# An attention-plus-MLP kernel on one core: the masked attention rebuilt in 64x64 quadrants of the matmul array

## The chip, the cores and the metric

The kernel runs on one core of one Trainium2 chip. The metric is the device time of one execution in microseconds (us), and a lower time is better. Times are medians of several executions. "Span" is the length of the one execution that the profiler recorded, a few us shorter than the time.

The profile names the engines PE (TensorE, matrix products), PEld (its weight loads), DVE (VectorE), ACT (ScalarE), POOL (GpSimd, which here issues the loads) and SP (SyncE, which here issues stores and transposes). `SPq` is SP's queue of DMA issues.

## The reference

There are eight batches with eight heads, 576 positions and a head size of 64. Heads 0 to 3 see a band of 32 keys, and heads 4 to 7 see every 32nd key. The result feeds two dense layers with a rational function between them.

```python
rel = pos[:, None] - pos[None, :]
mask_local   = (rel >= 0) & (rel < 32)                                   # heads 0..3
mask_strided = (rel >= 0) & (pos[None, :] % 32 == pos[:, None] % 32)     # heads 4..7
attn = softmax(where(mask, q @ k.T / 8, -1e9)) @ v
x = attn.transpose(0, 2, 1, 3).reshape(4608, 512)
h = x @ w_in                                                             # 512 -> 2048
P = a[0] + a[1] * h + a[2] * h**2 + a[3] * h**3
Q = 1.0 + abs(b[0]) * abs(h) + abs(b[1]) * h**2
out = (P / (Q + 1e-6)) @ w_out                                           # 2048 -> 512, float32
```

## The kernel before

The program records every operation with its engine, dependencies, a cost and a priority key. A list scheduler then fixes one static order for each engine. A ready operation with the lowest key goes first.

```python
for u in op.users:
    hop = 0.03 if (u.eng == e and op.group is None) else self.HOP    # gap before a dependent operation
    u.ready = max(u.ready, op.end + hop)
```

The tokens are cut into nine chunks of 512. Eight chunks hold the first 512 positions of one batch each, and the ninth holds the 64 left over from every batch. Attention of a batch passes in eleven rounds through one score tensor, `psS`, of two banks of PSUM, the memory where this program's matmuls put their results. Some rounds turn q and k with an identity product. The others add a mask (identity times mask, 128 columns wide) to the score products.

```python
psS = Pa("psS", [128, 2, 512], F32);  psA = Pa("psA", [128, 8, 128], F32)
psH = [Pa(f"psH{i}", [128, 512], F32) for i in range(3)];  psO = Pa("psO", [128, 512], F32)

def score_round(key, msk, width, qks, exps, deps, e_slot):
    for j in range(2):
        makers.append(mm(psS[:, j, 0:width], IDN[:, :], msk[:, 0:width], True, False))
    for (o, l, r) in qks:
        makers.append(mm(o, l, r, False, False))
    o1 = add("PE", makers, [deps, s_free[0], cons], cost, key)     # cons: all constants, one semaphore
```

The attention output goes to `XR`, is turned by a DMA transpose into `XT`, and feeds the first dense layer (`psH`). ACT copies that to `HB`. Nine DVE operations and two ACT ones make the rational function for a group of 512-token blocks. The second dense layer (`psO`) follows, then a copy to `OS` and the stores.

```python
for kk in range(NK1):
    r = XT[c % NXT][:, kk, :]
    makers.append(mm(psH[hi][:, :], Win[:, kk, 128 * f:128 * f + 128], r, kk == 0, kk == NK1 - 1))
o1 = add("PE", makers, [xt_ev[c], g1.ops, h_free[hi]], 4 * mmc(512), key)
# ... nine DVE operations; the polynomial's are a chain, each needs the one before:
d5 = add("DVE", ... t3 = t3 * hb ..., [d4], ctt, key + 0.04)
d6 = add("DVE", ... t3 = t3 + a1 ..., [d5], cts, key + 0.05)
d7 = add("DVE", ... t3 = t3 * hb ..., [d6], ctt, key + 0.06)
```

The softmax here doesn't subtract the row's maximum and nothing guards it: scores larger than these inputs give would overflow.

Of the kernel before, what the change touches and what calls it, by code (L numbers as in the profile page):

```python
# [4 lines left out]
dt = mybir.dt  # L5
# [6 lines left out]
STRIDE = 32  # L12
# [47 lines left out]
class Program:  # L60
# [32 lines left out]
    def schedule(self):  # L93
# [22 lines left out]
        while left:  # L116
# [34 lines left out]
            for u in op.users:  # L151
                hop = 0.03 if (u.eng == e and op.group is None) else self.HOP
                u.ready = max(u.ready, op.end + hop)
                u.nwait -= 1
                if u.nwait == 0:
                    heapq.heappush(future[u.eng], (u.ready, u.idx, u))
# [108 lines left out]
def bass_strided_sparse_attn__then__act_rational_pade_kernel(nc, q, k, v, moe_w_in, moe_w_out, moe_a, moe_b, out):  # L265
# [6 lines left out]
    NP = S // 4  # L272
    HL = 4
# [5 lines left out]
    P = 36.0  # L279
# [6 lines left out]
    qm = [A(f"qm{i}", [128, 256], BF) for i in range(NN)]  # L286
    km = [A(f"km{i}", [128, 256], BF) for i in range(NN)]
    sT = A("sT", [128, 2, 2, 4, NP], BF)
    qL = A("qL", [128, 2, S], BF)
    kL = A("kL", [128, 2, S], BF)  # L290
    NV = 2
    vt = [A(f"vt{i}", [128, 4, 4, VS], BF) for i in range(NV)]
    v4 = [A(f"v4{i}", [64, 4, VS], BF) for i in range(NV)]
    w4 = [A(f"w4{i}", [128, 4, VS], BF) for i in range(NV)]
    vs = [A(f"vs{i}", [128, 4, 4, VS], BF) for i in range(NV)]
    NE = 2
    EL1 = [[A(f"EL1_{i}_{p}", [128, 2, 4, 128], BF) for p in range(2)] for i in range(NE)]
    EL2 = [A(f"EL2_{i}", [128, 2, 2, 4, 4, 32], BF) for i in range(NE)]
    EL3 = [A(f"EL3_{i}", [64, 2, 2, 4, 32], BF) for i in range(NE)]
    ESW = 8 * NP + 64  # L300
    ES = [A(f"ES_{i}", [128, 2, ESW], BF) for i in range(NE)]
# [6 lines left out]
    XT8 = A("XT8", [128, NK1, B * 128], BF)  # L308
    NHB = 2
    HB = [A(f"HB{i}", [128, G, CH], BF) for i in range(NHB)]  # L310
    NT3 = 6
# [3 lines left out]
    NO = 4  # L315
    OS = [A(f"OS{i}", [128, 512], F32) for i in range(NO)]
# [4 lines left out]
    ML1 = A("ML1", [128, 512], BF)  # L321
    ML2 = A("ML2", [128, 384], BF)
    MS1 = A("MS1", [128, 3 * NP], BF)
    MS2 = A("MS2", [128, 2 * NP + 64], BF)
    IDN = A("IDN", [128, 128], BF)

    Pa = nc.alloc_psum_tensor
    psS = Pa("psS", [128, 2, 512], F32)
    psA = Pa("psA", [128, 8, 128], F32)
    NHP = 3  # L330
    psH = [Pa(f"psH{i}", [128, 512], F32) for i in range(NHP)]
    psO = Pa("psO", [128, 512], F32)


    ar = np.arange(128)
    part = np.arange(128)
    d1 = (4 * (ar % 32) + ar // 32)[None, :] - part[:, None]
    m1 = np.where((d1 >= 0) & (d1 < STRIDE), 0.0, NEG)
    ml1 = np.tile(m1, (1, 4))
    ml2 = np.full((128, 2, 4, 4, 8), NEG)  # L340
    ml3 = np.full((128, 2, 4, 16), NEG)
    for g in range(4):
        for i in range(16):
            dd = 4 * i + g - part
            ok = (dd >= 0) & (dd < STRIDE) & (part < 64)
            ml3[ok, :, g, i] = 0.0
            dd = 128 + 4 * i + g - part
            ok = (dd >= 0) & (dd < STRIDE)
            if i < 8:
                ml2[ok, :, :, g, i] = 0.0  # L350
            else:
                assert not ok.any()
    ml2 = np.concatenate([ml3.reshape(128, -1), ml2.reshape(128, -1)], axis=1)
    dp = np.arange(NP)[None, :] - part[:, None]
    ms = np.where((dp >= 0) & (dp % 8 == 0), 0.0, NEG)
    ms1 = np.tile(ms, (1, 3))
    iq = np.arange(16)[None, :]
    ik = (part % 32)[:, None]
    mlo = np.where((ik < 16) & (iq >= ik) & ((iq - ik) % 8 == 0), 0.0, NEG)
    ms2 = np.concatenate([np.tile(ms, (1, 2)), np.tile(mlo, (1, 4))], axis=1)  # L360
# [7 lines left out]
    nch = [0]  # L368
# [3 lines left out]


    gC = chan("c_const").group()
    cons = []
    for dst, arr, nm in ((IDN, np.eye(128), "c_idn"), (ML1, ml1, "c_ml1"), (ML2, ml2, "c_ml2"),
                         (MS1, ms1, "c_ms1"), (MS2, ms2, "c_ms2")):
        c = const(nm, arr)
        cons.append(add("SP", (lambda e, dst=dst, c=c: e.dma_start(dst.bitcast(dt.uint16)[:, :], c[:, :])),
                        [], 0.1, -900, gC, 0.1))  # L380
    cst_np = np.zeros((1, 2), np.float32)
    cst_np[0, 0] = 1.0 + 1e-6
    cst_c = nc.inline_tensor(cst_np, name="c_cst")
    cons.append(add("SP", lambda e: e.dma_start(
# [6 lines left out]
        coef[:, 6:8], coef[:, 4:6], -1.0, coef[:, 4:6], op0=Alu.mult, op1=Alu.max), [cons], 0.2, -400)  # L391
# [6 lines left out]

    ini = {}

    def memset(buf, ap, val, key=-800.0, eng="DVE", cost=0.3):
        o = add(eng, (lambda e, ap=ap, val=val: e.memset(ap, val)), [ini[id(buf)][-1]] if id(buf) in ini else [],
                cost, key)
        ini.setdefault(id(buf), []).append(o)

    for i in range(NV):
        memset(vt[i], vt[i][:, :, :, 64:65], 1.0)
        memset(vs[i], vs[i][:, :, :, 64:65], 1.0)
        memset(v4[i], v4[i][:, :, 64:65], 1.0)
        memset(w4[i], w4[i][:, :, 64:65], 1.0)  # L410
    for i in range(NE):
        memset(EL2[i], EL2[i].rearrange("x a q t g c -> x (a q t g c)"), 0.0, cost=1.2)
        memset(EL3[i], EL3[i].rearrange("x a q g c -> x (a q g c)"), 1.0)


    ch_n = [[chan(f"c_n{x}{i}") for i in range(NN)] for x in "qk"]
    ch_v = [chan(f"c_v{i}") for i in range(NV)]
    ch_x = [chan(f"c_x{i}") for i in range(NX)]
    ch_w1 = chan("c_w1")
    ch_w2 = chan("c_w2")  # L420
    ch_o = [chan(f"c_o{i}") for i in range(NO)]
    n_free = [[[] for _ in range(NN)] for _ in range(2)]
# [3 lines left out]
    g1 = ch_w1.group()  # L426
    g2 = ch_w2.group()

    def load_win():
        add("POOL", (lambda e: e.dma_start(Win[:, :, :], w_in.rearrange("(a p) f -> p a f", p=128))),  # L430
            [], 1.0, -940.0, g1, 12.0)

    def load_wout():
        add("POOL", (lambda e: e.dma_start(Wout[:, :, :], w_out.rearrange("(f p) o -> p f o", p=128))),
            [], 1.3, -920.0, g2, 12.0)

    def loads(b):

        key = (b - 2.5) * P if b > 1 else -1000.0 + 50 * b
        i = b % NN  # L440
        for x, src, dst, dsm in ((0, q, qn, qm), (1, k, kn, km)):
            g = ch_n[x][i].group()
            add("POOL", (lambda e, src=src, dst=dst, b=b, i=i: e.dma_start(
                dst[i][:, :, :], src[b, :, 0:512, :].rearrange("h (p g) d -> p h (g d)", g=4))),
                [n_free[x][i]], 0.9, key + x, g, 3.8)
            add("POOL", (lambda e, src=src, dsm=dsm, b=b, i=i: e.dma_start(
                dsm[i][:, :], src[b, :, 512:576, :].rearrange("h (p g) d -> h p (g d)", g=4))),
                [n_free[x][i]], 0.7, key + x + 0.1, g, 0.5)
            n_ev[x, b] = g.ops
        gv = ch_v[b % NV].group()  # L450
        i = b % NV
        base = [v_free[i], ini[id(vt[i])], ini[id(vs[i])], ini[id(v4[i])], ini[id(w4[i])]]
        key = (b - 1.9) * P if b > 1 else key + 5
        for h in range(4):
            add("POOL", (lambda e, b=b, i=i, h=h: e.dma_start(  # L455
                vs[i][:, h, :, 0:64],
                v[b, 4 + h, 0:512, :].rearrange("(p g) d -> p g d", g=4))),
                base, 0.85, key, gv, 1.1)
        for g in range(4):
            add("POOL", (lambda e, b=b, i=i, g=g: e.dma_start(  # L460
                w4[i][32 * g:32 * g + 16, :, 0:64],
                v[b, 4:8, 512:576, :].rearrange("h (p g) d -> g p h d", g=4)[g])),
                base, 0.65, key, gv, 0.15)
        for h in range(4):
            add("POOL", (lambda e, b=b, i=i, h=h: e.dma_start(  # L465
                vt[i][:, :, h, 0:64],
                v[b, h, 0:512, :].rearrange("(t p) d -> p t d", p=128))),
                base, 0.85, key, gv, 1.1)
        add("POOL", (lambda e, b=b, i=i: e.dma_start(
            v4[i][:, :, 0:64],  # L470
            v[b, 0:4, 512:576, :].rearrange("h s d -> s h d"))),
            base, 0.7, key, gv, 0.5)
        v_ev[b] = gv.ops


    s_free = [None]
    a_free = [None]
# [10 lines left out]
    def mmc(n):  # L488
        return max(n / 2.4, 28.0) * 1e-3 + 0.003

    def score_round(key, msk, width, qks, exps, deps, e_slot):
        makers = []
        nq = 0
        for j in range(2):
            makers.append(mm(psS[:, j, 0:width], IDN[:, :], msk[:, 0:width], True, False))
        for (o, l, r) in qks:
            makers.append(mm(o, l, r, False, False))
            nq += mmc(r.free_size())
# [3 lines left out]
        s_free[0] = o2  # L502
        return o2

    q_free = [[]]

    def evac(eng, dst, src, dep, key, n):
        if eng == "ACT":
# [414 lines left out]
```

## Time and profile before

The time before was 436.72 us (three runs, 436.19 to 440.19). The span has three parts:

| part | from | to | length |
|---|---|---|---|
| prologue: until the first dense matmul (`psH<-XT,Win`) | 0 | 69.9 | 69.9 |
| body: until the last operation of the rational function | 69.9 | 419.3 | 349.4 |
| tail: last dense products, copies, stores | 419.3 | 437.7 | 18.4 |

These lines are from the page of the kernel before: busy time by engine, then busy tenths in 40 slices of the span, with the clock that the throttle granted to TensorE.

```profile
PE 363.3 (83%) x3392; PEld 175.3 (40%) x3392; DVE 326.8 (75%) x307; ACT 307.1 (70%) x339; POOL 105.9 (24%) x142
PE   0446748896989699999999998999997999997950
DVE  2201301989799849499969999799988999999940
PEclk9999999985999999999999999999999999999995
```

PE and DVE both near 9 through most of the body mean that two engines are close to their limits at once. DVE does almost nothing in the first six slices.

The clock row misleads at its start. This trace's record of the clock begins at 73.0 us, and the view counts time without a record as full speed. The matmul starts tell otherwise. Up to 73 us, matmuls of 128 columns start 107 ns apart and the dense ones of 512 columns 427 ns; later it is 56 and 216 ns. So TensorE ran at half speed in the prologue, and the 1.00 in the first line below is not measured.

The windows view of the kernel before gives the same for the prologue and the body. Its columns are the stretch, its length, busy us of PE, PEld, DVE, ACT and POOL (with instructions), the clock, the DMA share and GB/s.

```profile
0.00:69.90 69.90, 32.77 (x428) 17.48 (x429) 12.06 (x31) 20.40 (x21) 40.15 (x61) 1.00 1.56 161
69.90:419.30 349.40, 326.88 (x2954) 156.31 (x2948) 313.40 (x274) 285.47 (x316) 65.78 (x81) 0.98 0.46 62
```

The chain of waits of the kernel before shows why the prologue is long. Each line is a start, a duration and what the chain passed through.

```profile
4.24 9.21 DMA coef<-in_moe_b_dram
13.59 1.02 PE psS L486 x8
14.64 1.24 DVE sT L510
16.01 1.03 PE psS L486 x8
17.06 1.03 ACT sT L509
...
44.29 8.45 DMA XT<-XR
...
68.33 1.64 PE psS L486 x17
69.97 3.33 PE psH L486 x8
```

The first score matmul waits for a small constant, because all constants share one semaphore. After that PE and an evacuation take turns on `psS` until 69.97, with an 8.45 us transpose between.

The timeline of the kernel before shows the tail. The line's columns are start, duration, engine, source line, operation, tiles and count.

```profile
421.05 14.87 SPq L806 DMA_DIRECT2D out_dram<-OS  x32
421.96 1.03 PE L486 MATMUL psS<-Wout,T 128*128 128x512 bf16 x4
```

The last matmul starts at 421.96, and 32 store issues keep the queue busy for 14.87 us.

### The profile page before, as it was taken

What the parts mean: (1) busy time and instruction counts of PE and PEld (TensorE: products, weight loads), DVE (VectorE), ACT (ScalarE), POOL (GpSimd) and SP (SyncE); (2) the same over time, 40 slices, a digit from 0 to 9 for tenths busy, and PEclk for the clock granted to TensorE, in tenths of its full rate; (3) what the DMA queues carried; (4) which work ended last, traced back from release to release, by engine and by line L of the source; (5) the groups of instructions that cost most, each with busy time, mean ns of one, the idle gap of its engine ahead of it and who ended that gap; (6) DMA issues with size and microseconds to landing.
All of it is one profiled execution on the core that took longest, in us unless ns stands there. A gap on an engine that the chain in (4) does not pass through costs nothing.

```text
span 437.7 us, 7910 instructions
## 1 busy us (share of the span) xinstructions
PE 363.3 (83%) x3392; PEld 175.3 (40%) x3392; DVE 326.8 (75%) x307; ACT 307.1 (70%) x339; POOL 105.9 (24%) x142
## 2 busy tenths in 40 slices
PE   0446748896989699999999998999997999997950
PEld 0223423442345255455544543555443444443420
DVE  2201301989799849499969999799988999999940
ACT  1152243768899777979698889898888499959520
POOL 9960091261101911900480009000000000000000
PEclk9999999985999999999999999999999999999995
DMA  8999999383503994952497228313111210112112
GB/s 120 175 184 196 172 120 130 46 60 40 70 13 74 179 40 61 151 81 67 57 103 121 49 49 80 57 31 77 28 41 31 67 49 25 48 26 54 42 32 65
DMA packets 92227, 34.03 MB, mean 78 GB/s; under 512 B 66080, under 2 KB 87072, under 8 KB 92192
## 3 DMA queue, kind: packets, MB, share of 16 engines
q0 software_dynamic: 62112, 18.37, 45.5%
q1 hardware_dynamic: 30080, 15.16, 16.6%
q8 instruction: 26, 0.43, 0.4%
q14 instruction: 9, 0.07, 0.1%
HBM read 37.17 MB, written 9.44 MB: 106 GB/s over the span
## 4 chain that ended last, share of the span: by engine, by line
PE 59%; DVE 16%; ACT 13%; DMA 6%; issue 2%; SPq 1%; DVEq 0%
PE psH L486 25%; PE psO L486 17%; PE psS L486 14%; ACT kL L509 4%; PE psA L486 4%; DMA XT<-XR 4%; DVE T L784 3%; DVE T L779 2%; ACT UU L765 2%; DMA coef<-in_moe_b_dram 2%; DVE UU L759 2%; DVE T L775 2%; ACT ES L582 1%; DVE T L777 1%; ACT HB L745 1%
## 5 line engine op out<-in xcount | busy, mean ns | idle before, releaser
L486 PE MATMUL psH<-XT,Win 128*128 128x512 bf16 x576 | 145.9, 391 | 4.1 <-DMA XT<-XR 2.1
L486 PE MATMUL psO<-Wout,T 128*128 128x512 bf16 x528 | 132.6, 380 | 9.2 <-ACT OS L849 7.0
L745 ACT ACTIVATE HB<-psH 128x512 bf16<-128x512 f32 x144 | 83.6, 604 | 36.1 <-PE psH L486 34.4
L486 PEld LDWEIGHTS psH<-XT,Win 128*128 128x128 bf16 x576 | 54.9, 100 | 70.6 <-issue 6.4
L765 ACT ACTIVATE UU<-UU,cst 128x2048 bf16<-128x2048 bf16 x36 | 71.9, 2001 | 8.1 <-DVE UU L759 8.1
L486 PEld LDWEIGHTS psO<-Wout,T 128*128 128x128 bf16 x528 | 47.1, 98 | 66.4 <-ACT OS L849 11.5
L768 ACT ACTIVATE UU<-UU 128x2048 bf16<-128x2048 bf16 x36 | 69.0, 1918 | 0.1
L455 POOL DMA_DIRECT2D vs<-in_v_dram x32 | 28.1, 884 | 103.1 <-PE psA L486 102.9
L784 DVE TENSOR_TENSOR T<-T,UU 128x4096 bf16<-128x4096 bf16 (+1 forms) x20 | 41.3, 2067 | 6.0 <-ACT UU L768 6.0
L775 DVE TENSOR_TENSOR T<-T,HB 128x4096 bf16<-128x4096 bf16 (+1 forms) x20 | 41.5, 2075 | 0.3
L759 DVE TENSOR_TENSOR UU<-UU,T 128x4096 bf16<-128x4096 bf16 (+1 forms) x20 | 41.5, 2073 | 0.3
L779 DVE TENSOR_TENSOR T<-T,HB 128x4096 bf16<-128x4096 bf16 (+1 forms) x20 | 41.4, 2071 | 0.2
L510 DVE CAST sT<-psS 128x1024 bf16<-128x1024 f32 (+1 forms) x16 | 13.2, 822 | 38.1 <-PE psS L486 38.1
L582 ACT ACTIVATE ES<-psS 128x864 bf16<-128x864 f32 (+1 forms) x24 | 20.3, 845 | 18.7 <-PE psS L486 18.5
L680 DVE TENSOR_TENSOR XR<-psA,RC 128x512 bf16<-128x512 f32 x40 | 27.5, 688 | 2.9 <-DMA XT<-XR 2.7
L753 DVE TENSOR_SCALAR T<-HB 128x4096 uint16<-128x4096 uint16 (+1 forms) x20 | 22.2, 1109 | 8.9 <-ACT HB L745 8.9
L678 DVE RECIPROCAL RC<-psA 128x8 f32<-128x8 f32 x40 | 8.2, 204 | 25.8 <-PE psA L486 25.7
L849 ACT ACTIVATE OS<-psO 128x512 f32<-128x512 f32 x33 | 19.7, 597 | 10.6 <-PE psO L486 10.1
L486 PE MATMUL psS<-ML,IDN 128*128 128x512 bf16 (+1 forms) x48 | 15.9, 418 | 13.5 <-ACT kL L509 9.0
L486 PE MATMUL psS<-IDN,qn 128*64 128x128 bf16 (+1 forms) x192 | 12.4, 254 | 17.5 <-DMA coef<-in_moe_b_dram 13.6
L465 POOL DMA_DIRECT2D vt<-in_v_dram x32 | 26.9, 870 | 0.0
L772 DVE TENSOR_SCALAR T<-HB,coef 128x4096 bf16<-128x4096 bf16 (+1 forms) x20 | 25.4, 1269 | 0.2
(77 smaller groups left out, 395.6 us busy)
## 6 DMA issues: line engine op xcount, KB each, us to landing
out_dram<-OS SPq DMA_DIRECT2D x128, 64.0 KB, 1.7
qn<-in_q_dram POOLq DMA_DIRECT2D x8, 512.0 KB, 6.4
kn<-in_k_dram POOLq DMA_DIRECT2D x8, 512.0 KB, 8.3
vs<-in_v_dram POOLq DMA_DIRECT2D x32, 64.0 KB, 6.0
vt<-in_v_dram POOLq DMA_DIRECT2D x32, 64.0 KB, 3.9
Win<-in_moe_w_in_dram POOLq DMA_DIRECT2D x1, 2048.0 KB, 14.7
Wout<-in_moe_w_out_dram POOLq DMA_DIRECT2D x1, 2048.0 KB, 26.3
out_dram<-OS SPq DMA_DIRECT2D x32, 32.0 KB, 1.7
```

The costliest lines, as they stand in the source:

```text
L455: add("POOL", (lambda e, b=b, i=i, h=h: e.dma_start(vs[i][:, h, :, 0:64], v[b, 4 + h, 0:512, :].rearrange("(p g) d -> p g d", g=4))), base ...
L465: add("POOL", (lambda e, b=b, i=i, h=h: e.dma_start(vt[i][:, :, h, 0:64], v[b, h, 0:512, :].rearrange("(t p) d -> p t d", p=128))), base, ...
L486: return lambda e: e.matmul(out_ap, l, r, start=start, stop=stop, skip_group_check=True)
L680: o3 = add("DVE", (lambda d, rc=rc, x=x: d.tensor_tensor(x.rearrange("x (h d) -> x h d", h=8), psA[:, :, 0:64], rc[:, :, :].to_broadcast([ ...
L745: o2 = add("ACT", (lambda a, hb=hb, hi=hi, fi=fi: a.activation(hb[:, fi, :], psH[hi][:, :], AF.Copy)), [o1, hb_free[ig % NHB]], 0.6, key - 30)
L759: d3 = add("DVE", (lambda d, gn=gn, u=u, t3=t3: d.tensor_tensor(u[:, 0:gn, :], u[:, 0:gn, :], t3[:, 0:gn, :], op=Alu.mult)), [d2], ctt, ke ...
L765: ln = add("ACT", (lambda a, u=u, sl=sl: a.activation(u[:, sl, :], u[:, sl, :], AF.Ln, bias=cst[:, 0:1], scale=1.0)), [d3, cons], 0.28 + H ...
L768: ex = add("ACT", (lambda a, u=u, sl=sl: a.activation(u[:, sl, :], u[:, sl, :], AF.Exp, scale=-1.0)), [ln], 0.28 + HG * CH * 0.000833, key ...
L772: d4 = add("DVE", (lambda d, gn=gn, hb=hb, t3=t3: d.tensor_scalar(t3[:, 0:gn, :], hb[:, 0:gn, :], a_ap[3], a_ap[2], op0=Alu.mult, op1=Alu. ...
L775: d5 = add("DVE", (lambda d, gn=gn, hb=hb, t3=t3: d.tensor_tensor(t3[:, 0:gn, :], t3[:, 0:gn, :], hb[:, 0:gn, :], op=Alu.mult)), [d4], ctt ...
L779: d7 = add("DVE", (lambda d, gn=gn, hb=hb, t3=t3: d.tensor_tensor(t3[:, 0:gn, :], t3[:, 0:gn, :], hb[:, 0:gn, :], op=Alu.mult)), [d6], ctt ...
L784: d9 = add("DVE", (lambda d, gn=gn, t3=t3, u=u: d.tensor_tensor(t3[:, 0:gn, :], t3[:, 0:gn, :], u[:, 0:gn, :], op=Alu.mult)), [d8, lns], c ...
```

## The change

The change rebuilds attention in 64x64 quadrants of the array and rearranges what surrounds it. Its parts are these:

- Masks are products of one-hot matrices of 64 rows, four quadrants a set, in place of 128-wide masks.
- q and k are turned by PSUM transposes in bf16, so that one copy takes 2048 elements.
- PSUM becomes four sets of two banks (S, A, H, O). Batch 0 and batch 1 spread over all of them.
- Loads are reordered and split: strided heads first, `Win` in two halves, a semaphore for each constant.
- The token order in `XT` changes, so the dense layer reads its moving operand in short runs.
- Groups at the start and end get smaller, one `T3` buffer goes, stores go by 64 partitions, and the scheduler's gap for the same engine goes from 0.03 to 0.

```diff
-                hop = 0.03 if (u.eng == e and op.group is None) else self.HOP
+                hop = 0.0 if (u.eng == e and op.group is None) else self.HOP
...
-    P = 36.0
+    P = 34.0
+    SB, AB = 1.4, 0.0
...
-    NT3 = 6
+    NT3 = 5
...
-    psS = Pa("psS", [128, 2, 512], F32)
-    psA = Pa("psA", [128, 8, 128], F32)
-    psH = [Pa(f"psH{i}", [128, 512], F32) for i in range(NHP)]
-    psO = Pa("psO", [128, 512], F32)
+    PS = {n: Pa("ps" + n, [128, 2, 512], F32) for n in "SAHO"}
...
+    def quads(ps, col, w, mcol, rhs, start):
+        for c in range(2):
+            for r in range(2):
+                res.append(mm(ps[64 * c:64 * c + 64, r, col:col + w],
+                              MK[64 * r:64 * r + 64, mcol + 64 * c:mcol + 64 * c + 64], rhs[r], start, False))
...
+                            makers.append(tp(pb[:, x, o:o + 128], T[:, 4 + h, 128 * gh:128 * gh + 128], IDN[:, :]))
...
-        return [4, 4, 8] if c == 0 else [8, 4, 4] if c == NCH - 1 else [8, 8]
+        return [2, 2, 4, 8] if c == 0 else [8, 4, 2, 2] if c == NCH - 1 else [8, 8]
...
-                        r = XT[c % NXT][:, kk, :]
+                            if kk < 2:
+                                r = xt[:, kk, :].rearrange("x (s c r) -> x c s r", c=8, r=4)
+                            else:
+                                r = xt[:, kk, :].rearrange("x (s c r) -> x c s r", c=8, r=32)
...
-                        dst[g], OS[osl][64 * bb + 16 * g:64 * bb + 16 * g + 16, :])), [ev], 0.45, key - 60, go, 0.1)
+                src = OS[osl][64 * z:64 * z + 64, e_, :]
...
+                    dst = out[r0:r0 + 64, :].rearrange("(i g) o -> g i o", g=4)
```

## The prediction

> **What bounds the kernel now.** The span is 437.7 us, in three parts (timeline view).
> 1. *Prologue, 0 to 69.9 us*, before the first dense matmul (group psH<-XT,Win). PE is busy 33 of the first 70 us, DVE 12 (windows view). The first score matmul starts at 13.59, released by the coefficient load, because all constants share one semaphore. Eleven rounds per batch then pass one by one through the single two-bank score tensor: batch 0 to about 41, batch 1, ahead of dense work on PE, to about 70. An XT transpose takes 8.45 us in the chain of waits, against a median of 2.7.
> 2. *Body, 70 to 419*. From 175 to 315 PE is busy 34.3 of each 35 us; from 245 to 420 DVE is 32.5 to 34.6. Dense PE work is 1152 x 0.216 = 249 us, attention about 11 us per batch (start-to-start: mask pairs 0.47, attend tiles 0.45 to 0.9); DVE's rational function is about 275 us plus 5.6 per batch.
> 3. *Tail, 419 to 437.7*: the last matmul starts at 421.96, but 32 stores issued one after another, 0.42 us each, last until 435.9.
>
> **What the change does.**
> - Prologue: K and Q in halves, Win in halves, constants split, dense 0 in groups of two, rounds spread over four PSUM sets. The packet records show batch 0's first half of q/k landed at 9.0 us, all at 15.1, v at 19.1, Win 26.1 to 38.9. I expect attend tiles from about 20 us, transposes slowed by loads to about 8, and the first dense matmul at about 36 (30 to 44): 34 us saved, all critical.
> - Body: attention goes from 280 to 392 matmuls per batch, but in small quadrants. The trace has sixteen 128*32 matmuls in 0.24 us (15 ns each), 128-column ones at about 30 ns. With 20 ns for quadrants and 0.43 us per mask set I estimate 9.7 us against 11.1. The Trainium skill ("TensorE: Matmul & The Clock Gate", Part 3) says matmuls in distinct tiles run concurrently; I count part of that. DVE: the sT casts (1.24 us for 1024 fp32 elements) become one bf16 cast of 2048 in about 1.2; about 1 us less per batch. ACT: 144 evacuations of 604 ns become 72 of 1.04; kL's 2.45 becomes about 1.03; some 30 us less, off the critical path. Body 349 to about 340: PE and DVE each still need about 305.
> - Tail: 8 stores for 32, last group of two: 18 to about 9 us.
>
> Sum: 36 + 340 + 9 = 385.
>
> **Predicted: 386 us, 80% range 370 to 405. Chances: faster 0.96, same 0.02, slower 0.02.**
>
> **What would show it.** First psH matmul near 36; about 4300 PE matmuls; PE busy about 345, ACT 280, DVE 322; dense matmuls still 216 ns apart although their moving operand is read in runs of four elements; OS stores ending within 7 us of the last matmul; DVE at 33 or more of 35 through the body.
>
> **What would make it wrong.** Dense matmuls slowed by the strided moving operand (each 10% costs 12 us). One psH set for three banks: ACT's 2 us Ln and Exp ahead of an evacuation may stall PE. R2 writes PSUM with a step of four; the Trainium skill ("PSUM — Partial Sum Buffer", Specifications) says non-contiguous patterns slow matmuls. Mask quadrants might serialise. Transposes might wait longer behind loads, and V needs two on-chip copies before the first attend tile.

## The result, and the profile after

The changed kernel is correct. It took 416.37 us (415.36 to 417.48, four runs) beside 436.46 for the kernel before on the same chip (435.7 to 440.19). The ratio is 0.9516, with a 95% interval of 0.9458 to 0.9575.

The change is faster, but by 20 us where the prediction said 50. The profiled execution splits as follows.

| part | before | predicted | after | miss |
|---|---|---|---|---|
| prologue | 69.9 | 36 | 43.25 | +7 |
| body | 349.4 | 340 | 353.6 | +14 |
| tail | 18.4 | 9 | 16.8 | +8 |
| sum | 437.7 | 385 | 413.6 | +29 |

The same lines of the page after:

```profile
PE 329.8 (80%) x4320; PEld 167.1 (40%) x4320; DVE 329.7 (80%) x304; ACT 263.3 (64%) x229; POOL 157.5 (38%) x215
PE   0621892879977999999998998999699699699930
DVE  2121388985788788989999998989999998999940
PEclk9955797789989999999999999999999899999975
```

PE fell by 33 us, more than the 18 that the prediction promised (to 345), and yet DVE's busy time rose a little. PE shows gaps in the last third (6s and 9s), where DVE is at 9. Early on the clock is at half: 5, 5, 7, 9, 7, 7. That is no step down from the kernel before, whose 9s there are not measured (its record begins at 73.0 us; here it begins at 15.5).

The windows view after, for prologue and body:

```profile
0.00:43.25 43.25, 10.52 (x297) 8.58 (x297) 9.38 (x27) 4.34 (x4) 40.96 (x65) 0.72 1.49 155
43.25:396.80 353.55, 316.54 (x4016) 157.73 (x4016) 319.08 (x276) 257.96 (x224) 116.56 (x150) 0.96 0.63 79
```

In the body PE went from 327 to 317 and DVE from 313 to 319, where the prediction gave both about 305.

The chain of waits after, at the prologue:

```profile
16.07 7.24 DMA VL<-VL
25.01 9.99 DMA XT<-XR
35.74 7.46 DMA XT<-XR
43.25 3.35 PE psH L521 x8
...
65.64 5.23 DMA XT<-XR
```

The attend tiles were ready at 24 us, as predicted ("from about 20"). In the chain, two transposes in a row then took 9.99 and 7.46 us from issue to landing. Only three `XR` buffers exist, so the fourth tile waits for the first transpose. The first eight dense matmuls took 3.35 us after that wait, where eight take 1.73 later on. The Trainium skill ("TensorE: Matmul & The Clock Gate", Part 1) says that about 3.4 us without work halves the clock. The trace agrees: TensorE had sat idle for 9.4 and then 5.5 us with 16 short matmuls between, 3.35 is 1.9 times 1.73, and the profile's clock row has 5 in the slices just before. But the change did not bring this cost: in the chain of the kernel before, the first eight took 3.33 us, at half speed as well.

The timeline after, at the tail:

```profile
397.76 1.89 PE L521 MATMUL psS<-Wout,T 128*128 128x512 bf16 x4
399.03 5.73 SPq L917 DMA_DIRECT2D out_dram<-OS  x8
```

The eight issues end at 404.8, but by the trace's packet records the last packet ends at 412.8.

Two things that the prediction marked as risks turned out harmless. The timeline after, in the middle of the body:

```profile
94.97 1.89 PE L521 MATMUL psH<-XT,Win 128*128 128x512 bf16 x8
96.69 1.89 PE L521 MATMUL psO<-Wout,T 128*128 128x512 bf16 x8
...
104.98 0.41 PE L521 MATMUL psS<-IDN,MK 64*64 64x512 bf16 x4
105.22 0.42 PE L521 MATMUL psS<-sT 64*64 64x64 bf16 x32
```

Eight dense matmuls with the strided moving operand took 96.69 - 94.97 = 1.72 us, so 215 ns each, and the short runs cost nothing. Four mask quadrants of 512 columns took 105.22 - 104.98 = 0.24 us from start to start, hardly more than one dense matmul of 512 columns. So they ran together, as the Trainium skill ("TensorE: Matmul & The Clock Gate", Part 3) says of matmuls in distinct tiles. The estimate of 0.43 us was too high, and the error lay on the safe side.

A third risk came true. The turn of k (`R2` in the code) now writes PSUM with a step of four. The same 16 matmuls of 128 columns, both at full clock, the kernel before first:

```profile
140.95 0.64 PE L486 MATMUL psS<-IDN,kn 128*64 128x128 bf16 x16
```

```profile
139.18 1.06 PE L521 MATMUL psS<-IDN,kn 128*64 128x128 bf16 x16
```

From the first start to the last, they took 0.418 us before and 0.750 after, 1.8 times as long. That agrees with the page on PSUM that the prediction names. It costs TensorE about 0.4 us for each batch, some 3 us in all.

### A ledger for DVE

A cut at the first dense matmul hides one thing: work that was in the prologue can move into the body. I therefore use a second account over the whole run. The time at which the rational function ends is DVE's occupied time plus its idle time before that. A gap of 0.1 us or more between two DVE instructions is idle here, counted in the stretch where it ends, and everything else is occupied. All numbers are worked out from the start times and durations in the traces.

| kernel | rational function ends | DVE occupied | DVE idle | of it, 0-50 / 50-90 / 90-190 / later |
|---|---|---|---|---|
| before | 419.3 | 327.7 | 91.6 | 38.3 / 25.4 / 17.9 / 9.9 |
| after | 396.8 | 335.2 | 61.7 | 37.9 / 2.8 / 16.5 / 4.5 |

The change removed 30 us of DVE idle time, mostly between 50 and 90 us, and added 7.5 us of DVE occupation. Predicted was a fall of some 8 us in occupation. The idle time of the first 50 us hardly changed.

### The profile page after: what moved, and what is told of

Its sections match the earlier page's. It is cut to its first block, busy times and chain, and to the rows that moved or that the text cites. A ratio compares the mean times of both kernels' runs of the same rounds, so it can differ in the third digit from the quotient of the medians.

```text
span 413.6 us, 9670 instructions
## 1 busy us (share of the span) xinstructions
PE 329.8 (80%) x4320; PEld 167.1 (40%) x4320; DVE 329.7 (80%) x304; ACT 263.3 (64%) x229; POOL 157.5 (38%) x215
## 4 chain that ended last, share of the span: by engine, by line
DVE 38%; PE 33%; DMA 11%; ACT 9%; issue 4%; POOL 1%; SPq 0%; DVEq 0%; ACTq 0%; POOLq 0%
PE psH L521 14%; PE psO L521 12%; DMA XT<-XR 7%; DVE UU L871 6%; DVE T L896 5%; DVE T L887 4%; DVE T L891 4%; PE psS L521 4%; DVE UU L868 4%; ACT UU L877 3%; DVE T L884 3%; DVE XR L780 3%; ACT UU L880 3%; DVE T L865 3%; PE psA L521 3%
## 5 line engine op out<-in xcount | busy, mean ns | idle before, releaser
L521 PE MATMUL psH<-XT,Win 128*128 128x512 bf16 x480 | 117.9, 388 | 15.6 <-DMA XT<-XR 8.0
L856 ACT ACTIVATE HB<-psH 128x1024 bf16<-128x1024 f32 x68 | 69.3, 1020 | 82.0 <-PE psH L521 79.5
L877 ACT ACTIVATE UU<-UU,cst 128x2048 bf16<-128x2048 bf16 (+1 forms) x38 | 72.6, 1910 | 10.3 <-DVE UU L871 10.2
L880 ACT ACTIVATE UU<-UU 128x2048 bf16<-128x2048 bf16 (+1 forms) x38 | 69.2, 1822 | 0.5
L470 POOL DMA_DIRECT2D VT<-in_v_dram x64 | 46.7, 804 | 0.0
L896 DVE TENSOR_TENSOR T<-T,UU 128x4096 bf16<-128x4096 bf16 (+2 forms) x22 | 41.7, 1896 | 3.5 <-ACT UU L880 3.2
L887 DVE TENSOR_TENSOR T<-T,HB 128x4096 bf16<-128x4096 bf16 (+2 forms) x22 | 41.9, 1903 | 0.7
L871 DVE TENSOR_TENSOR UU<-UU,T 128x4096 bf16<-128x4096 bf16 (+2 forms) x22 | 41.9, 1903 | 0.6
L891 DVE TENSOR_TENSOR T<-T,HB 128x4096 bf16<-128x4096 bf16 (+2 forms) x22 | 41.8, 1902 | 0.6
L458 POOL DMA_DIRECT2D VL<-in_v_dram x32 | 28.3, 924 | 32.0 <-PE psA L521 32.0
L889 DVE TENSOR_SCALAR T<-T,coef 128x4096 bf16<-128x4096 bf16 (+2 forms) x22 | 24.2, 1100 | 0.7
L894 DVE TENSOR_SCALAR T<-T,coef 128x4096 bf16<-128x4096 bf16 (+2 forms) x22 | 24.0, 1091 | 0.7
L780 DVE TENSOR_TENSOR XR<-psA,RC 128x512 bf16<-128x512 f32 (+1 forms) x36 | 22.7, 632 | 1.2
L778 DVE RECIPROCAL RC<-psA 128x8 f32<-128x8 f32 (+1 forms) x36 | 7.0, 196 | 18.5 <-PE psA L521 18.4
```

The costliest lines, as they stand in the source:

```text
L470: add("POOL", (lambda e, h=h, c=c: e.dma_start(VT[i][64 * c:64 * c + 64, h, :, 0:64], v[b, 4 + h, 0:512, :].rearrange("(x c g) d -> c x g ...
L521: return lambda e: e.matmul(out_ap, l, r, start=start, stop=stop, skip_group_check=True)
L780: o3 = add("DVE", (lambda d, rc=rc, x=x, src=src, nh_=nh_: d.tensor_tensor(x[:, 0:64 * nh_].rearrange("x (h d) -> x h d", h=nh_), src[:, : ...
L856: o2 = add("ACT", (lambda a, hb=hb, ps=ps, fi=fi: a.activation(hb[:, fi:fi + 2, :], ps[:, :, :], AF.Copy)), [o1, hb_free[ig % NHB]], ca(10 ...
L871: d3 = add("DVE", (lambda d, gn=gn, u=u, t3=t3: d.tensor_tensor(u[:, 0:gn, :], u[:, 0:gn, :], t3[:, 0:gn, :], op=Alu.mult)), [d2], ctt, ke ...
L877: ln = add("ACT", (lambda a, u=u, sl=sl: a.activation(u[:, sl, :], u[:, sl, :], AF.Ln, bias=cst[:, 0:1], scale=1.0)), [d3, cons], 0.28 + H ...
```

## The experiments

All runs below were checked against the reference. Those meant to give a wrong result say so. Runs of one group shared a chip and the kernel before. Between groups I compare ratios. "Ends" is again the end of the rational function in the profiled execution.

### 1. The scheduler's gap

Theory: with the gap at 0, the scheduler places a DVE operation directly behind the one it depends on, because the dependent one is ready as early as any other. In the static DVE order of the kernel before, 63 neighbours depend on each other, and in the changed one 178. Two timelines show what that does. First, the kernel before:

```profile
332.30 1.28 DVE L777 TENSOR_SCALAR T<-T,coef 128x4096 bf16<-128x4096 bf16 x1
333.49 0.20 DVE L678 RECIPROCAL RC<-psA 128x8 f32<-128x8 f32 x1
333.61 2.29 DVE L779 TENSOR_TENSOR T<-T,HB 128x4096 bf16<-128x4096 bf16 x1
335.82 0.68 DVE L680 TENSOR_TENSOR XR<-psA,RC 128x512 bf16<-128x512 f32 x1
```

Then the changed kernel:

```profile
334.36 2.29 DVE L887 TENSOR_TENSOR T<-T,HB 128x4096 bf16<-128x4096 bf16 x1
336.69 1.29 DVE L889 TENSOR_SCALAR T<-T,coef 128x4096 bf16<-128x4096 bf16 x1
338.01 2.29 DVE L891 TENSOR_TENSOR T<-T,HB 128x4096 bf16<-128x4096 bf16 x1
```

Before, the small attention operations sit between the members of the chain, and an instruction starts before its predecessor's recorded end: 333.61 + 2.29 is 335.90, and the next starts at 335.82. After, each starts 0.03 to 0.04 us behind the end: 334.36 + 2.29 is 336.65, and the next starts at 336.69.

The gap applies to every engine, so the orders of the others can change with it. The edits are below. The changed kernel ran once more as a control.

```diff
 a_hop03, from the changed kernel:        b_hop0, from the kernel before:
-  hop = 0.0  if (u.eng == e ...)        -  hop = 0.03 if (u.eng == e ...)
+  hop = 0.03 if (u.eng == e ...)        +  hop = 0.0  if (u.eng == e ...)
```

The control:

> The changed kernel again, as the reference point on this chip. Every theory expects 415 to 418 us, with the dense start at about 43 us, the last rational-function operation ending at about 397 and the end at about 414 in the trace.

The gap restored in the changed kernel:

> The changed kernel with the old 0.03 us same-engine gap in the list scheduler. By the schedules, DVE instructions that follow directly on the one they depend on fall from 178 to 89 (before: 63). Theory (a directly dependent DVE instruction starts about 0.125 us later than an independent one, and the change's 0.0 gap made the scheduler stop interleaving): DVE work falls by some 11 us, the body from 353.6 to about 343, time about 405 us (402 to 410); overlapping pairs in the trace rise from 86 to above 150. Rival (the body is held by the single psH set and ACT's order, and the dependent starts fall into slack): 413 to 418.

Gap taken from the kernel before:

> The kernel before with the gap set to 0.0, nothing else. Dependent neighbours on DVE rise from 63 to 159. Theory: 96 x 0.125 = 12 us more DVE work, of which at least the part from 245 us on, where DVE is full, shows: 441 to 449 us. Rival (order on DVE is of no account): 434 to 438.

| run | time | ratio [95%] | ends | DVE occupied | DVE idle |
|---|---|---|---|---|---|
| a_same | 417.84 | 0.9529 [0.9429, 0.9629] | 396.1 | 335.8 | 60.3 |
| a_hop03 | 414.5 | 0.9461 [0.9372, 0.9551] | 394.5 | 324.4 | 70.1 |
| before | 440.99 | 1 | 419.3 | 327.7 | 91.6 |
| b_hop0 | 441.64 | 1.0074 [0.9988, 1.016] | 422.0 | 339.4 | 82.7 |

(The times and ratios are of this group's chip. "Ends" and the ledger of the kernel before are those of its one kept trace, from the group before, with 436.72 us as its median.)

The effect on DVE is as the theory says, in both directions: 11.4 and 11.7 us of occupation. The effect on the time is not. Of that, 1.6 and 2.7 us reached the end, and idle time took the rest. The 402 to 410 us that the theory expected of a_hop03 were missed; its 414.5 lies in the rival's range. The ratios' intervals overlap, so the small time effect itself is not settled by these runs.

I then measured the disputed cost alone: a kernel with nothing but DVE products of 128x4096 elements, twelve in one chain and then twelve in two chains taken in turn. It computes nothing of the reference.

> Wrong result on purpose: DVE alone, first twelve 128x4096 bf16 products in one chain, each waiting for the one before it, then twelve in two chains taken in turn, each waiting for the last but one. Theory: start to start about 2.32 us in the chain and 2.20 when alternating, 0.12 apart. Rival (what looked like a cost of dependence is a cost of something else in the kernels, such as the other engines' traffic): the same distance in both parts.

The start times in its trace lie 2.327 us apart in the first part and 2.202 us apart in the second. The lines view of two windows of this run, one inside each part, gives durations in busy us and mean ns:

```profile
L21 DVE TENSOR_TENSOR X<-X,Y 128x4096 bf16<-128x4096 bf16 x11 | 25.2, 2293 | 0.4
L21 DVE TENSOR_TENSOR X<-X,Y 128x4096 bf16<-128x4096 bf16 x12 | 26.5, 2282 | 0.0
```

The durations are alike (2293 and 2282 ns). The cost is in when the next one may start: 0.125 us for each instruction that waits for its direct predecessor. Dependent neighbours went from 178 to 89 in a_hop03 and from 63 to 159 in b_hop0. At 0.125 us each that makes 11.1 and 12.0 us, an estimate from these numbers, and the ledgers show 11.4 and 11.7. This mechanism is settled.

### 2. The last stores

Theory: the tail is long because the last stores use only four DMA engines. In the last 512 packets of 2 KB, the packet records show 4.0 in flight at once, and they last 12.5 us, 84 GB/s. A 256-packet store late in the body lasts 2.7 us with 14 in flight, 195 GB/s. The destination of a last store is `(i g) o -> g i o`, whose first dimension is 4. The Trainium skill ("DMA: Bandwidth & Descriptors", "Why a DMA increments its semaphore by 16 and not by 1") says that a transfer is shared by the largest number of engines, up to 16, that divides the slowest dimension of both sides. With 64 partitions on one side and 4 on the other, that is 4.

The edit makes 16 stores whose both sides have 16 in front:

```diff
-   dst = out[r0:r0 + 64, :].rearrange("(i g) o -> g i o", g=4)            # [4, 16, 512] from 64 partitions
+   rows = out.rearrange("(b r) o -> r b o", r=576)
+   src = OS[osl][64 * z + 16 * g:64 * z + 16 * g + 16, :, :]
+   dst = rows[512 + g:576:4, 4 * i2 + z:4 * i2 + z + 3:2, :]              # [16, 2, 512] from 16 partitions
```

> The changed kernel with the last eight stores (64 partitions against a destination whose outer dimension is 4) cut into sixteen of 16 partitions x 2 rows, one for each g. Theory (the outer dimension of 4 lets each store use 4 DMA engines only; the trace has exactly 4.0 packets in flight, 14 in the other stores): more than 8 packets in flight, the last packet ends about 8 us after the first in place of 12.5, time 411 to 413 us. Rival (the write to memory is limited at about 84 GB/s in that pattern, or the issue of more stores costs as much as it saves): 415 to 418.

It took 411.46 us (ratio 0.9404 [0.9305, 0.9502]), 6.4 us under its control, and was correct. The span fell from 412.8 to 406.7. The queue line of this run and its last packets:

```profile
397.29 7.37 SPq L914 DMA_DIRECT2D out_dram<-OS  x16
```

Twice the issues keep the queue busy a little longer than the 5.73 us of the eight. But the last 512 packets now take 7.7 us with 12.4 in flight. So it was not the number of issues that mattered, and the rival, a limit of 84 GB/s on writing these rows, is out: they were written at 136. The tail is now 11.6 us, and 2.6 us of the predicted 9 stay unexplained by this.

### 3. The prologue: a fourth buffer, or fewer loads in the way

Two causes of the late dense start are at hand. One is that three `XR` buffers make the fourth tile wait. The other is that the transposes share the DMA engines with the loads, which move 106 to 203 GB/s in the slices of those 40 us.

```diff
 a_nx4:   -  NX = 3      +  NX = 4
 a_hold:  the loads after batch 1's q and k get one more dependency:
+          held[0] = list(xt_ev[0])      # the transposes of batch 0
-          [n_free[x][part][i]], 0.9, key, g, 1.95)
+          [n_free[x][part][i], held[0]], 0.9, key, g, 1.95)
```

> The changed kernel with four XR buffers in place of three, so that batch 0's fourth tile need not wait until the first transpose (10 us) has landed. Theory (two causes: the transposes move behind the loads, and the fourth one starts 8 us late for want of a buffer): the fourth XR ends at about 27 in place of 35.7, the four transposes land together at 37 to 41, dense start 38 to 41 in place of 43; time 1 to 5 us less. Rival (the loads alone set when transposes land, whenever they were issued): dense start unchanged at 43.

> The changed kernel with every load after batch 1's four q/k halves held until batch 0's four transposes have landed. Theory (a transpose is slow because the loads' packets stand before it): the first transpose lands within about 5 us of its issue in place of 10, dense start at about 33 to 36 in place of 43. The held loads then come later and may cost something afterwards, so the time is 408 to 416. Rival (transposes are slow at this point for another reason, such as their own descriptors): first transpose still takes 8 to 10 us, dense start 41 or later.

With a fourth buffer the first dense matmul came at 40.3. The time stayed (418.68, ratio 0.9531 [0.944, 0.9622]). With the loads held it came at 33.0. The transposes' queue lines of the changed kernel and of a_hold, from the timelines:

```profile
25.01 11.93 SPq L795 DMA_TRANSPOSE XT<-XR  x4
```

```profile
25.09 6.66 SPq L798 DMA_TRANSPOSE XT<-XR  x4
33.00 2.61 PE L524 MATMUL psH<-XT,Win 128*128 128x512 bf16 x8 [0.46 <-DMA XT<-XR]
```

The four transposes are issued within 6.66 us in place of 11.93 and take 2.4 to 4.7 us to land in place of 7.5 to 12.4. TensorE's wait for the first `XT` went from 5.5 to 0.5 us. But its wait for batch 1's `XT` rose from 2.5 to 8.0. So loads in the way made 10 of the 43 us, and the prediction's 36 was within reach. But the time was 413.16 (ratio 0.9431 [0.9346, 0.9516]) and the rational function ended at 393.9. Of the 10 us, 2 to 3 reached the end.

All four edits together (gap, stores, buffer, loads) were the next run:

> All four edits together: 0.03 us gap, sixteen last stores, four XR buffers, held loads. If the losses add, dense start about 33, the tail 11 us, time 400 to 408 us; if the body is held by something none of them touches and the earlier start is given back, 408 to 412.

It started dense work at 31.8 and took 411.29 us (one of its four runs, 415.8, was slow; the median of the other three is 409.48), ratio 0.9368 [0.9274, 0.9462]. That is correct and faster than the changed kernel, but no faster than the sum of the stores and the gap would make it. The progress of the rational function, read from the trace as the time when a number of its 144 blocks of 128 features by 512 tokens are done, shows where the start was lost:

| run | first dense | 16 | 32 | 48 | 64 | 96 | 144 |
|---|---|---|---|---|---|---|---|
| before | 69.9 | 129.6 | 162.1 | 208.5 | 251.3 | 331.8 | 419.3 |
| a_same | 42.5 | 89.2 | 140.6 | 186.3 | 226.7 | 295.1 | 396.1 |
| a_hop03 | 43.3 | 89.0 | 138.1 | 190.8 | 230.6 | 297.3 | 394.5 |
| a_hold | 33.0 | 89.5 | 146.2 | 191.3 | 227.2 | 296.3 | 393.9 |
| a_all | 31.8 | 88.3 | 145.0 | 196.6 | 231.2 | 298.8 | 395.9 |

By block 16 an earlier start of 10 us has vanished.

### 4. Is it TensorE that takes back what DVE gains?

If both engines are near their limit, then relieving one alone shows little. To test it, half of the second dense layer's matmuls are left out (a wrong result), with the order on every engine kept.

```diff
-    for kk in range(q0, q0 + 4):
+    for kk in (q0, q0 + 3):
         makers.append(mm(ps[:, e_, :], gl(res[kk], 2 * i2 + e_), Wout[:, kk, :], ...))
```

> Wrong result on purpose: the changed kernel with half of the matmuls of the second dense layer left out (576 of 1152 dense ones stay there halved to 288), same instruction order on every engine. About 62 us of TensorE work go. Theory (TensorE and VectorE both need about 316 of the body's 353 us and each waits for the other): with TensorE light, VectorE alone bounds the body, so the body falls to VectorE's own 326 us or so plus 10 to 15 us of waits: time about 400, 14 to 18 us less. Rival (VectorE alone bounds the body, TensorE never did): time falls by under 6 us.

> Wrong result on purpose: the same lighter second dense layer, in the kernel with the scheduler's gap put back to 0.03. Theory (the 10 us of VectorE time that the gap gave back were eaten by waits for TensorE): with TensorE light, they now show, so this run is 8 to 11 us faster than a_peless0, against 1 to 3 us between the two full kernels. Rival (the gap's VectorE time is lost in another way, for instance waits for ScalarE or DMA): again only 1 to 3 us.

| | gap 0: ratio, ends, occupied + idle | gap 0.03: ratio, ends, occupied + idle |
|---|---|---|
| all of TensorE's work | 0.9529, 396.1, 335.8 + 60.3 | 0.9461, 394.5, 324.4 + 70.1 |
| without half of the second layer | 0.9506, 397.3, 335.7 + 61.6 | 0.931, 387.2, 324.4 + 62.8 |

(The last chunk's own loop was left alone, so 256 matmuls went rather than the 288 of the expectation: 55 us at 0.216 each.)

The first expectation failed. With gap 0, 55 us less work for TensorE changed nothing (ratio 0.9506 [0.9442, 0.957]). As far as this test goes, the changed kernel is bounded by DVE and by waits that the second dense layer has no part in. (TensorE ran slower in it, as shown below.) The second expectation came true: with TensorE light, the gap's 11 us on DVE are worth 10 us at the end, against 1.6 with TensorE's full work (8.1 against 3.3 in the times). Only with both engines relieved was the gain large. The likely reading is that TensorE lies only about 2 us behind DVE, so that a lighter DVE at once waits for it. The wait records bear this out only in part. From 49 us on, DVE waited 31.6 us in a_hop03 and 23.2 in a_same. Of these 8 us more, 6 were for ACT's copies `HB` of the first dense layer (13.7 against 7.8), and they stayed with TensorE light (13.2). What fell then were the waits for TensorE itself (`psA` and `psS`, from 13.3 to 7.4). The gap also moved attention: its last transpose starts at 299.0 in a_hop03 and at 288.0 in a_same. So ACT, the single `psH` set or the changed orders may take a part of the 11 us; no run separates them. The windows of these two runs, over the same stretch, gap 0 first:

```profile
43.00:397.00 354.00, 284.85 (x3760) 135.78 (x3760) 319.33 (x276) 257.29 (x224) 117.44 (x150) 0.89 0.64 79
```

```profile
43.00:397.00 354.00, 280.91 (x3768) 135.10 (x3768) 313.00 (x277) 256.99 (x225) 115.96 (x150) 0.91 0.63 80
```

PE's busy time at gap 0 fell by 28 us (312.99 in the control), not by 55, and the granted clock fell too, from 0.96 to 0.89. Busy time times clock gives 300 and 254 us, 46 less, near the 55 removed. The first dense layer's matmuls, which were all kept, lay 248 ns apart on average in place of 226. A test that lightens an engine is thus weaker than it looks.

### 5. Why an earlier start is given back

In a_all, TensorE waits for batch 1's transposes. The same wait in the run with more loads held is below it. Both are from timelines:

```profile
73.44 3.60 PE L524 MATMUL psH<-XT,Win 128*128 128x512 bf16 x8 [11.43 <-DMA XT<-XR]
```

```profile
62.48 3.59 PE L526 MATMUL psH<-XT,Win 128*128 128x512 bf16 x8 [6.06 <-DMA XT<-XR]
```

The second is a_hold2, where `Wout`, small loads and batch 2's loads wait for batch 1's transposes as well. The second dense layer had to be recorded before the first: five `T3` buffers otherwise allowed chunk 1 to overwrite what chunk 0 had not used.

```diff
+   held[0] = list(xt_ev[1])     # then Wout, the small loads of batches 0 and 1, batches 2..7
-   if 1 <= step <= NCH: res[step - 1] = dense1(step - 1)
    if step >= 2:        dense2(step - 2, res[step - 2])
+   if 1 <= step <= NCH: res[step - 1] = dense1(step - 1)
```

> a_all, with Wout, the small loads and all of batch 2's loads held until batch 1's transposes have landed (and the second dense layer's record made before the first's, which a dependency needs). Theory (batch 1's transposes waiting behind loads give back the earlier start): TensorE's 11.4 us wait for XT of batch 1 falls under 3 us, block 16 leaves the rational function near 78 to 82 us instead of 88, time 4 to 8 us under a_all's ratio of 0.937, so near 0.92. Rival (the next limit, VectorE and TensorE in 90 to 190 us, takes it back as well): block 16 comes earlier, the end moves by under 3 us.

A rival idea was that attention, whose last transpose starts at 289 us in the changed kernel and at 300.4 in a_all, crowds the early body and leaves DVE alone in the last third:

```diff
-    SB, AB = 1.4, 0.0
+    SB, AB = 1.0, -0.4
```

> a_all, with the attention of batches 2 to 7 given a later priority on every engine (0.4 of a chunk later for scores and attend tiles), so that it spreads over more of the body. Theory (attention is finished at 289 us and so crowds TensorE before 190 us while VectorE alone works after 290): the last transposes come 10 us or more later, VectorE idle time in 90 to 190 us falls, time falls by 4 to 8 us. Rival (the total of both engines' work decides, not its order): the last transposes move and the time stays within 2 us of a_all's, or rises because XT is late.

And two runs took away about three quarters of the load bytes of batches 2 to 7 (wrong; the loads of v are cut likewise, not shown):

```diff
-    big[i][:, h0:h0 + 4, :], src[b, h0:h0 + 4, 0:512, :] ...
+    big[i][:, h0:h0 + (4 if b < 2 else 1), :], src[b, h0:h0 + (4 if b < 2 else 1), 0:512, :] ...
```

From a_all:

> Wrong result on purpose: a_all with the q, k and v loads of batches 2 to 7 cut to about a quarter of their bytes; instructions and their order stay. Theory (those loads, by holding batch 1's transposes and the later batches' data, give back the earlier dense start): TensorE's wait for XT in 30 to 190 us falls from 19.5 to under 8, VectorE idle in 50 to 190 us from 37 to under 20, block 48 leaves near 180 instead of 197, and the time falls by 10 to 18 us, to a ratio near 0.90. Rival (TensorE and VectorE themselves bound that stretch): time within 4 us of a_all's 411.

From a_hold2:

> Wrong result on purpose: a_hold2 (loads held for batch 1's transposes as well) with the q, k and v loads of batches 2 to 7 cut to a quarter as in a_light. Theory (the early start is given back to loads alone): block 16 leaves the rational function near 78 us as in a_hold2 and now stays ahead, block 48 near 175 to 178, the rational function ends 8 to 12 us before a_light's 387.5, time near 388. Rival (TensorE and VectorE bound the stretch once loads are light): block 16 early, but block 48 near a_light's 187 and the time within 4 us of 398.

| run | time | ratio [95%] | first dense | 16 | 48 | ends | DVE idle, 50-90 / 90-190 |
|---|---|---|---|---|---|---|---|
| a_all | 411.29 | 0.9368 [0.9274, 0.9462] | 31.8 | 88.3 | 196.6 | 395.9 | 11.8 / 25.4 |
| a_hold2 | 422.27 | 0.965 [0.9569, 0.9732] | 31.8 | 77.4 | 203.3 | 405.2 | 7.2 / 39.9 |
| a_late | 413.07 | 0.9401 [0.9305, 0.9498] | 32.1 | 90.1 | 189.8 | 400.6 | 12.1 / 22.7 |
| a_light | 398.5 | 0.912 [0.9044, 0.9195] | 31.6 | 88.7 | 186.9 | 387.5 | 11.2 / 17.8 |
| a_hold2_light | 415.27 | 0.9487 [0.9412, 0.9563] | 32.1 | 78.1 | 198.5 | 400.2 | 7.0 / 33.6 |

- The first loss, before block 16, is batch 1's transposes. Freed of loads, they took 2.5 to 4.1 us in place of 9.2 to 13.6 and brought block 16 forward by 11 us, though the wait halved rather than vanished.
- The second loss is later. In a_all the loads of later batches cost 8 us at the end (395.9 to 387.5 in a_light), and 0.025 of the ratio, so 11 us of time. DVE idle time in 50 to 190 us fell by 8 us, not to the 20 that I had expected. TensorE's wait for batch 1's `XT` did not move (11.1 us). So the loads of batches 2 to 7 do not cause that one, and a_hold2 points to `Wout` and the small loads, which it held back and a_light did not cut.
- Both together did not add. My theory that loads alone give the start back fell: a_hold2_light is slower than a_light. Waits of a_hold2 in 77 to 205 us, by engine and releaser (us in total, times, longest):

```profile
DVE RC L783 <- PE psA L526: 26.1, 7, 5.1
POOL VL L460 <- PE psA L526: 14.0, 3, 9.4
DVE T L870 <- PE psO L526: 9.7, 1, 9.7
```

The held `Wout` delays the second dense layer, and the five `T3` buffers pass that on to DVE (`T <- psO`). Attention of the next batches then comes late (`RC <- psA`). a_hold2 also changed the order in which the two dense layers are recorded, and no run tests that alone. How much an arrangement without this stall would gain stays open.
- Moving attention later did not help. The last transpose started at 312.4 in place of 300.4, as expected, and the ratio is no better than a_all's (0.9401 against 0.9368, overlapping intervals). Its profiled execution was slow, so I don't lean on its ledger.

### 6. The two small edits together

> The changed kernel with two lines' worth of edits, the 16-partition last stores (6 us alone) and the scheduler's gap of 0.03 (2 us alone). If the two add, near 408 to 409, ratio 0.932 to 0.935, no slower than a_all; if they don't add, near 411.

The changed kernel with the 16-partition stores and the gap of 0.03 took 409.2 us (408.83 to 409.63), ratio 0.9358 [0.9277, 0.9439], correct. That beats both kernels, needs neither held loads nor the fourth buffer, and is as good as a_all. Its rational function ends at 395.6, so most of its gain over the changed kernel is in the tail.

## Why the prediction was wrong

The direction was right and the size was not: 386 predicted, 416.37 measured, outside of the range of 370 to 405. The three terms of the sum were all too small.

1. **"First dense matmul at about 36" was 43.25.** The text allowed "transposes slowed by loads to about 8". There were two in a row, 9.99 and 7.46 us, because of the three `XR` buffers. The buffer alone is worth 2 to 3 us (40.3), and the loads in the way 10 (33.0).
2. **"All critical" failed more than the 36.** Starting dense work 10 us earlier ended the rational function only 2 to 3 us earlier. The prediction added a prologue and a body as if they were independent. But batch 1's attention, its transposes and the loads behind it do not vanish when dense work starts before them; they move into the body. The ledger says it without a boundary: the change removed 30 us of DVE idle time, not 34 us of prologue and something more.
3. **"Body 349 to about 340: PE and DVE each still need about 305" is the term with the largest miss.** DVE was occupied for 325.2 of the body's 353.6 us (28.4 idle, less than the 35 that the prediction implied). Of the 20 us between 305 and 325.2, about 2 are the measure: the kernel before had 313.4 us busy, but 315.4 occupied by the ledger's rule. About 11 are the first hunk of the diff, which the prediction never costed: the gap of 0 put dependent DVE operations behind each other. The remaining 7 are a saving that did not show inside the body. Over the whole run the casts and the rest saved 3.3 us with the gap restored (327.7 to 324.4), where 8 were predicted, and part of batch 1's attention now falls into the body (DVE busy time in the prologue went from 12.06 to 9.38). Its marks, "DVE 322" against 329.7 and "DVE at 33 or more of 35", count busy time and can hardly tell occupation from work.
4. **Undoing that step alone returns 2 us at the end (3 in the time), not 11**. With TensorE light it returns 10 (8 in the time). So the body's miss has no single owner: DVE's extra occupation, what lies just behind it (TensorE by the likely reading, ACT's copies by a part of the waits), and the early waits for transposes and loads (16 of the 24 us that DVE idled after its first rational operation lie in 90 to 190 us).
5. **"Tail 18 to about 9" was 16.8.** The count of stores fell to 8 as foreseen. Their shape was not checked: 4 engines instead of 16, worth 5 us of the tail (16.7 to 11.6) and 6 of the time. The mark "OS stores ending within 7 us of the last matmul" failed, with the last packet 15 us after that matmul's start.

Of the risks that the prediction named, two did not occur: the moving operand in short runs (215 ns) and the mask quadrants (0.24 us for four). "Transposes might wait longer behind loads" did. So did the strided PSUM write of the k turn, though it is small (1.8 times as long, some 3 us of TensorE in all). For the single `psH` set TensorE waited 11.0 us in all, 2.0 in the kernel before; what this cost at the end was not tested. PE's busy time (329.8 against 345) and ACT's (263 against 280) came out better than predicted, and the time did not follow.

The account is not closed. The fastest correct kernel here took 409.2 us, 23 above the prediction. With most of the load bytes of batches 2 to 7 gone, a_light still took 398.5.

## What to carry to other kernels

Before crediting a change with an engine's saved time, find the engine that is next behind and by how much: here DVE's 11 us were worth 2 until TensorE was lightened, and 10 afterwards. Check a clock row against the matmul starts before comparing two traces by it. Keep one account over the whole run (occupied plus idle time of the busiest engine) beside a cut into phases, because work slips over the cut. Read the small lines of a diff, too: a scheduler constant and the outermost dimension of eight stores, neither part of the rebuilt attention, made 7 of the 30 us of the miss (416.4 to 409.2).

## What the Trainium skill lacked or had wrong

- "VectorE: DVE Perf Modes", "The DRAIN you can't avoid", measures that a semaphore after each copy costs nothing. It gives no cost for waiting on the instruction directly before. Here that wait cost 0.125 us an instruction (2.327 against 2.202 us from start to start, 128x4096 bf16 products), and in a whole kernel 11 to 12 us.
- "DMA: Bandwidth & Descriptors", "Why a DMA increments its semaphore by 16 and not by 1", has the rule for the number of engines, and the trace agrees (4.0 packets in flight). The section names no cost beside it; the page's Specifications list a bandwidth per engine, about 27 GiB/s, which would make an estimated 116 GB/s of four. Here it was 84 GB/s with 4.0 packets of 2 KB in flight against 195 with 14, and 6 us of this kernel.
- The same page, "DMA Transpose (X-bar)", gives no duration under load. The first four transposes of 128x512 bf16 tiles took 7.5 to 12.4 us to land among the loads and 2.4 to 4.7 us with the later loads held back.
- "TensorE: Matmul & The Clock Gate", Part 1, puts the warm-up below 1% of a typical kernel and describes, separately, how waits for DMA bring the low clock back. The second fits the changed kernel: its clock is recorded at half from 18.9 to 46.2 us, with idle times of 5.9, 9.4 and 5.5 us in or at the edge of that stretch. But the warm-up is no small thing here: the kernel before ran at half speed until 73.0 of its 437.7 us, with TensorE busy for 33 of the first 70. Nor does Part 1 say what this does to an experiment that takes matmuls away: with 256 of them gone the mean clock fell to 0.89, and busy time by 28 us rather than 55.
- "SBUF — State Buffer", Specifications (TRN2), asks for at least two hits in each 16-byte line for full bandwidth. Runs of four bf16 elements agree with it (215 ns for 512 columns); the page has no such figure for TensorE's moving operand.
